# Transnormer attention and SoLU feed-forward on one core: chunk 5 on token rows, its scaling on GpSimd, and a new order of the pieces

## The chip, the cores and the metric

The kernel runs on one core of one Trainium2 chip. The metric is the device time of one execution in microseconds (us). Before the change it is 182.4 us, the median of three runs (181.66 to 182.57).

The core has five engines that run at once: TensorE (PE in the profile, with its weight loads shown apart as PEld), VectorE (DVE), ScalarE (ACT), GpSimd (POOL) and SyncE (SP), which here only issues transfers. Transfers run on 16 DMA engines; SP, ACT and POOL each have a queue for issuing them. The on-chip memory that all engines read is SBUF; matmuls write to PSUM, of which this kernel uses three slots of two banks (P0 to P2) and two slots of one bank (S0, S1).

## The reference

The inputs are q, k and v of shape (8, 8, 576, 64) (batch, head, position, head size). What is computed:

```
kv  = einsum('bhsd,bhse->bhde', k, v)            # one 64x64 matrix per head
o   = einsum('bhsd,bhde->bhse', q, kv)
x   = o / sqrt(mean(o*o over the 64) + 1e-6) * g_norm   # -> 4608 tokens x 512
h   = x @ w_in                                    # 512 -> 1024
u   = h * softmax(h)
y   = (u - mean(u)) / sqrt(var(u) + 1e-6) * g_ln
out = y @ w_out                                   # 1024 -> 512, float32
```

## The kernel before

The 4608 tokens are cut into nine chunks of 512. Chunks 0 to 7 are the first eight of the nine position groups of each batch; chunk 8 gathers the ninth group of all batches (`q_last`, filled by the copies `ql0` to `ql7`). Every chunk goes through the same stages, each a named piece:

- loads `k`, `v`, `q` (POOL queue, cast from float32 to bfloat16 under way; `k0a` and `v0a` come over SP and ACT and are cast by `cast0.0` and `cast0.1`). The number is the batch; `a` and `b` are the halves of batches 0 and 1;
- `kv` on PE makes the 64x64 matrices, `kc...` copies them to SBUF (`kvd`) in three parts: straight, and the two row halves swapped;
- q is turned, by PE (`qt`, copied out by `qc`) for chunks 0 to 4, by a DMA transpose on SP (`qx`) for chunks 5 to 8;
- `o` multiplies q with the matrices. For chunks 0 to 5 o comes out with features on partitions: `sq` squares it (ACT), `s` averages it over a head on PE, `ln` and `ex` give the reciprocal root (ACT), `x` scales (DVE). For chunks 6 to 8 (`ROWS_OF_X`) o comes out with tokens on partitions: `sq` (ACT), a row sum `vd` (DVE), two small ACT instructions `vl`, the spread of the scale factor `vg` (POOL, 128x1024), `x` (DVE, reads o from PSUM), and a DMA transpose `xt` on SP;
- `h` is the first big matmul; `e` the exponential (ACT), `u` the product (DVE). Chunks 0 to 2 keep features on partitions, with `r` (squares), `g` (sums) and the PE sums `z`. Chunks 3 to 8 have tokens on partitions: `e` and `u` give their sums along the way, `r` squares u for its sum (ACT or DVE), and `t` turns u by a DMA transpose on SP;
- `st` and `rs` make the last row factor, `a` is the second big matmul, `b` scales its result into a result buffer `ob` (ACT or DVE), `d` stores it.

All DMA transposes wait for `gate`, a one-element copy on POOL that needs the last load, `q7`.

The order is a table (`ORDER`) in which every piece stands once, with the buffer it takes after @ (M0 to M12 of 4.6 KB, L0 to L7 of 9.2 KB, `ob` of 2 KB a partition) and its engine after /. Each engine runs its own pieces in table order; waits between engines come from the data and the buffers. So a piece that is not ready holds up everything behind it on its engine or queue, and nothing else directly.

Lines in the profile: L314 `kv`, L359 `qt`, L370 `qx`, L407 `o` on features, L470 `o` on rows, L435 `s`, L495 `vg`, L504 `x` on rows, L483 `vd`, L512 `xt`, L572 and L581 `h`, L599 `e` on rows, L612 `u` on rows, L630 and L632 `r` on rows (ACT and DVE), L637 `t`, L767 and L774 `a`, L782 and L784 `b`, L173 and L175 copies by ACT and the others, L343 `gate`, L269 the loads, L714 to L720 the row statistics `st`.

Of the kernel before, what the change touches and what calls it, by code (L numbers as in the profile page):

```python
# [68 lines left out]
warm0@S0 k0a@L0,L1 v0a rsqrt q0a@M0 k0b ident qt0.0@S0 cast0.0/act cast0.1/dve kv0a@P0 kc0a.1/act v0b q0b wi0  # L69
kc0a.2/act gr warm1@S1 tg@S1 qc0.0/dve@M1 kc0a.0/act o0.0@P0 sq0.00@osq0 sq0.01@osq1 warm2@S0 kv0b@P1 kc0b.0/act  # L70
kc0b.1/dve s0.00@S0 ex0.00@rst0 kc0b.2/act qt0.1@P2 qc0.1/dve s0.01@S0 ex0.01@rst1 warm3@P1 o0.1@P2 sq0.10@osq1
sq0.11@osq0 warm4@S0 s0.10@S0 warm5@P1 gm@M2 x0.00@M1 ex0.10@rst0 s0.11@S1 x0.01 x0.10 ex0.11@rst1 x0.11 wi1
h0.0+@P0 wo0@L2 h0.1+ h0.2+@P1 h0.3+ h0.0 h0.1 h0.2 wo1@L3 table e0.0@M3 u0.0@L1 h0.4+@P2 k1a@L0 h0.5+ v1a h0.3 h0.4
# [784 lines left out]
```

## Time and profile before

The profiled execution took 181.77 us and spans 179.7 us from the first to the last instruction; 2.07 us lie around the span. The granted TensorE clock is 0.999.

| engine | busy us of 179.7 | instructions |
|---|---|---|
| PE | 164.9 | 1808 |
| PEld | 81.1 | 1831 |
| ACT | 128.1 | 239 |
| DVE | 127.1 | 222 |
| POOL | 71.9 | 83 |

The DMA engines moved 37.81 MB in 60424 packets. In the page's rows of 40 slices a digit is the busy share of a slice of 4.5 us in tenths. PE's matmuls overlap by some 160 ns each (379 ns from start to end, 216 ns from start to start), so that a group's time is not its count times its mean.

### The profile page before, as it was taken

The page shows a single profiled execution, that of the slowest core. Times are in us where ns is not written, and L with a number is a line of the kernel's source. Part 1 is how long each engine was busy: PE and PEld are TensorE (multiplying, and loading weights), DVE is VectorE, ACT ScalarE, POOL GpSimd, SP SyncE. Part 2 cuts the span into 40 slices and gives each one's busy share as a digit, 9 for nine tenths or more (in the row PEclk, how much of TensorE's full clock was granted, in tenths as well). Part 3 has the DMA queues.
Part 4 walks back from the last instruction along what each step waited for, and adds up shares of the span by engine and source line. Part 5 has one row for each costly group of instructions (what it writes and reads, how often), then busy time and mean ns, then how long its engine had stood idle before and what let it go on. Part 6 is the DMA issues. An engine that isn't in the chain of part 4 may idle for free.

```text
span 179.7 us, 4520 instructions
## 1 busy us (share of the span) xinstructions
PE 164.9 (92%) x1808; PEld 81.1 (45%) x1831; DVE 127.1 (71%) x222; ACT 128.1 (71%) x239; POOL 71.9 (40%) x83
## 2 busy tenths in 40 slices
PE   6899958699999999999998999899999999999990
...
ACT  2377794593899687979879898469979746986210
...
DMA  5999999999999999999799999999998689968994
GB/s 170 252 207 275 353 208 209 205 208 222 248 233 232 209 207 198 277 214 206 157 172 203 206 216 220 152 256 245 171 227 239 99 166 248 200 139 215 175 256 125
DMA packets 60424, 37.81 MB, mean 210 GB/s; under 512 B 42140, under 2 KB 55204, under 8 KB 60404
## 3 DMA queue, kind: packets, MB, share of 16 engines
...
## 4 chain that ended last, share of the span: by engine, by line
PE 63%; DMA 22%; DVE 6%; issue 3%; POOL 1%; SPq 1%; ACT 1%; POOLq 0%; DVEq 0%; ACTq 0%
PE ps_S L767 20%; PE ps_P L581 19%; DMA sb_M<-in_q_dram 9%; PE ps_P L572 8%; PE ps_P L767 5%; DMA out_dram<-sb_ob 4%; DMA sb_L<-in_v_dram 4%; DMA sb_M<-sb_M 3%; PE ps_S L359 2%; DVE sb_ob L784 2%; PE ps_P L314 2%; PE ps_P L407 2%; DMA sb_L<-sb_L 2%; PE ps_P L691 1%; PE ps_S L435 1%
## 5 line engine op out<-in xcount | busy, mean ns | idle before, releaser
L767 PE MATMUL ps_S<-w_out_sb,sb_L 128*128 128x512 bf16 x220 | 53.1, 379 | 2.9 <-issue 2.4
L581 PE MATMUL ps_P<-w_in_sb,sb_M 128*128 128x512 bf16 x188 | 42.7, 379 | 1.0 <-ACT kvd L173 0.8
L767 PEld LDWEIGHTS <-sb_L 128*128 128x128 bf16 x280 | 26.4, 98 | 33.4 <-issue 3.3
L612 DVE SCALAR_TENSOR_TENSOR sb_L<-ps_P,sb_M 128x1024 bf16<-128x1024 f32 x24 | 29.1, 1222 | 8.4 <-ACT sb_M L599 8.2
L599 ACT ACTIVATE sb_M<-ps_P 128x1024 f32<-128x1024 f32 x24 | 24.5, 1023 | 8.2 <-PE ps_P L581 7.1
L581 PEld LDWEIGHTS <-sb_M 128*128 128x128 bf16 x192 | 18.7, 98 | 23.3 <-issue 0.9
L495 POOL TENSOR_TENSOR sb_M<-rr,g_rep 128x1024 f32<-128x1024 f32 x6 | 12.3, 2061 | 30.4 <-ACT rr L491 23.7
L572 PE MATMUL ps_P<-sb_M,w_in_sb 128*128 128x512 bf16 x94 | 21.9, 379 | 0.1
L607 DVE TENSOR_TENSOR sb_L<-ps_P,sb_M 128x1024 bf16<-128x1024 f32 x12 | 14.6, 1222 | 8.2 <-ACT sb_M L592 8.2
L453 DVE SCALAR_TENSOR_TENSOR sb_M<-ps_P,g_cols,sb_rst 128x512 bf16<-128x512 f32 x24 | 18.0, 790 | 2.9 <-ACT sb_rst L443 2.6
L784 DVE TENSOR_SCALAR sb_ob<-ps_S,rstd 128x512 f32<-128x512 f32 (+1 forms) x19 | 13.8, 735 | 7.7 <-PE ps_S L767 2.2
L592 ACT ACTIVATE sb_M<-ps_P 128x1024 f32<-128x1024 f32 x12 | 12.2, 1024 | 6.9 <-PE ps_P L572 6.9
L643 POOL TENSOR_TENSOR sb_M<-sb_M 128x512 bf16<-128x512 f32 x12 | 15.1, 1278 | 4.9 <-ACT sb_M L592 4.8
L420 ACT ACTIVATE sb_osq<-ps_P 128x512 bf16<-128x512 f32 x24 | 13.4, 596 | 4.6 <-PE ps_P L407 4.6
L630 ACT ACTIVATE sb_M<-sb_L 128x1024 bf16<-128x1024 bf16 x14 | 14.6, 1047 | 0.0
L572 PEld LDWEIGHTS <-w_in_sb 128*128 128x128 bf16 x96 | 9.2, 98 | 10.5 <-issue 0.2
L801 POOL DMA_DIRECT2D out_dram<-sb_ob x10 | 6.3, 633 | 16.4 <-DVE sb_ob L784 8.8
L632 DVE SCALAR_TENSOR_TENSOR sb_M<-sb_L 128x1024 bf16<-128x1024 bf16 x10 | 12.8, 1276 | 0.1
L443 ACT ACTIVATE sb_rst<-sb_lss 128x512 f32<-128x512 f32 x20 | 12.0, 632 | 0.1
L767 PE MATMUL ps_P<-w_out_sb,sb_L 128*128 128x512 bf16 x47 | 11.4, 379 | 0.1
L206 PE MATMUL ps_S<-zeros 128*128 128x512 bf16 (+1 forms) x18 | 8.5, 591 | 1.8 <-DVE zeros L188 1.5
L624 POOL TENSOR_TENSOR sb_L<-sb_L 128x1024 bf16<-128x1024 bf16 x4 | 7.6, 1910 | 6.1 <-DVE sb_L L607 6.0
...
## 6 DMA issues: line engine op xcount, KB each, us to landing
out_dram<-sb_ob SPq DMA_DIRECT2D x14, 256.0 KB, 4.2
sb_L<-in_k_dram POOLq DMA_DIRECT2D x6, 576.0 KB, 12.2
sb_L<-in_v_dram POOLq DMA_DIRECT2D x6, 576.0 KB, 13.1
sb_M<-in_q_dram POOLq DMA_DIRECT2D x6, 576.0 KB, 12.3
out_dram<-sb_ob POOLq DMA_DIRECT2D x10, 256.0 KB, 4.8
...
```

What stands on the lines that cost most here:

```text
L420: nc.scalar.activation(out=t[:, :], in_=T["o", c, hf][:, z], func=AF.Square)
L453: nc.vector.scalar_tensor_tensor(out=T["x", c][:, pairs_of(c, hf), :, z], in0=T["o", c, hf][:, z].rearrange("p (n q) -> p n q", n=2), scal ...
L572: nc.tensor.matmul(t[:, f % 2], w_in_sb[:, dt, f * 128:(f + 1) * 128], T["x", c][:, dt].rearrange("p q z -> p (q z)"), start=(dt == 0), st ...
L581: nc.tensor.matmul(T["h", c, m][:, half], x_block(c, m, dt), w_in_sb[:, dt, half * 512:half * 512 + 512], start=(dt == 0), stop=(dt == NP ...
L599: nc.scalar.activation(out=t.rearrange("p a b -> p (a b)"), in_=T["h", c, m].rearrange("p a b -> p (a b)"), func=AF.Exp, accum_out=T["zsum ...
L607: nc.vector.tensor_tensor(out=flat(T["u", c][:, 2 * p:2 * p + 2, :]), in0=flat(T["h", c, p]), in1=flat(T["e", c, p]), op=MUL)
L612: nc.vector.scalar_tensor_tensor(out=T["un", c][:, m, :], in0=T["h", c, m].rearrange("p a b -> p (a b)"), scalar=1.0, in1=T["e", c, m].rea ...
L630: nc.scalar.activation(out=unused, in_=src, func=AF.Square, accum_out=by)
L632: nc.vector.scalar_tensor_tensor(out=unused, in0=src, scalar=1.0, in1=src, op0=MUL, op1=MUL, accum_out=by)
L643: nc.gpsimd.tensor_tensor(out=T["es", c][:, n, :], in0=e[:, 0, :], in1=e[:, 1, :], op=ADD)
L767: nc.tensor.matmul(T["acc", c, m][:, 0], T["u", c][:, f, m * 128:(m + 1) * 128], w_out_sb[:, f, :], start=(f == 0), stop=(f == NF - 1))
L784: nc.vector.tensor_scalar_mul(out=t[:, :], in0=src, scalar1=T["rstd", c][:, m:m + 1])
```

## The change

- `ROWS_OF_X` takes in chunk 5: its o, x and transpose take the token-row way.
- On token rows, x no longer reads PSUM. A new piece `oc` (ACT or DVE) copies o to an SBUF tile in float32, and `x` becomes a GpSimd multiplication of that tile with the spread factor.
- `kvd` becomes three tiles, one for each of the three copies.
- The row squares `r` of chunks 3 to 8 run on ACT only; the copies `ql` on POOL or ACT only; the row statistics `st` of chunks 3 to 8 become six small GpSimd multiplications and additions in place of four DVE instructions. The constants they need are two new small tiles.
- There are 9 instead of 8 L buffers and 11 instead of 7 result buffers.
- The order table is new throughout. By its engine marks, ten row squares leave DVE for ACT, two squares of chunks 0 to 2 leave ACT for POOL, `b` goes from 14 on ACT and 23 on DVE to 10 and 27, both first casts are on DVE, `ql` goes from 3 POOL, 3 DVE and 2 ACT to 5 POOL and 3 ACT, `oc` is 7 times on DVE and once on ACT. Loads 2 to 7 stand earlier, the first store (`d0.0`) stands behind the last load.

```diff
-SLOTS = {"P": 3, "S": 2, "L": 8, "M": 13, "osq": 4, "lss": 3, "rst": 4, "ob": 7}
+SLOTS = {"P": 3, "S": 2, "L": 9, "M": 13, "osq": 4, "lss": 3, "rst": 4, "ob": 11}
-ROWS_OF_X = (6, 7, 8)
+ROWS_OF_X = (5, 6, 7, 8)
 ORDER = """
...
-r0.1/act u0.2 u0.3 r0.2/act r0.3/act wm1 wc4 kv1a@P2 kc1a.1/act kc1a.0/act warm6@S0 qt1.0@S0 z0@P0 warm7@P1
-kc1a.2/act wc1 wc2 qc1.0/act@M1 o1.0@P2 warm8@S0 wc3 sq1.00@osq0 sq1.01@osq1 kv1b@P1 kc1b.1/act kc1b.2/act wc5 wc0
-wc7 y0 a0.00@S0 wc6 q1b k2@L5 v2 ql0/pool q2@M2 k3@L4 st0 rs0 qt1.1@S1 kc1b.0/dve s1.00@P0 s1.01@P1 ln1.00@lss0
...
-d0.0/pool q3@M1 s1.10@S0 ln1.10@lss1 x1.00@M7 x1.01 s1.11@P1 ln1.11@lss0 h1.0+@P2 h1.1+ ex1.10@rst0 x1.10
-ex1.11@rst1 x1.11 a0.20@S0 kv2@P1 kc2.1/dve kc2.2/dve a0.21 h1.0 h1.1 b0.1/act@ob1 d0.1/sp qt2.0@S1 kc2.0/dve
...
+ex0.10@rst2 x0.10 ex0.11@rst0 table x0.11 h0.0 h0.1 h0.2 h0.3 h0.4+@P1 h0.5+ h0.4 h0.5 wm0@S0 wm1 e0.0@M1 e0.1@M4
+u0.0@L1 k1a@L0 h0.6+@P0 v1a q1a@M5 k1b u0.1 e0.2@M6 h0.6 u0.2 h0.7+ h0.7 r0.0/act@L4 wc5 v1b q1b kv1a@P1 warm6@S1
+r0.1/act e0.3@M3 wc1 wc4 kc1a.0/act kc1a.2/act wc0 qt1.0@S1 warm7@P2 wc7 qc1.0/dve@M2 kc1a.1/act o1.0@P1 sq1.00@osq1
+sq1.01@osq0 u0.3 g0.0@M7 g0.1 warm8@S1 kv1b@P2 kc1b.1/act wc2 k2@L5 v2 q2@M4 k3@L6 wc6 s1.00@S1 s1.01@P0 wc3 g0.2
+kc1b.0/act ln1.00@lss0 ln1.01@lss1 ex1.00@rst0 ql0/act kc1b.2/dve r0.2/pool a0.00@S0 qt1.1@S1 g0.3 qc1.1/dve
+ex1.01@rst2 r0.3/pool z0@P0 x1.00@M0 y0 o1.1@P2 x1.01 a0.01 sq1.10@osq0 s1.10@S1 sq1.11@osq1 s1.11@P1 ln1.10@lss1
+ln1.11@lss0 st0 kv2@P0 kc2.0/dve a0.10@S1 a0.11 ex1.10@rst2 ex1.11@rst0 v3 q3@M3 k4@L2 v4 q4@M2 k5@L4 rs0 h1.0+@P1
...
+a1.00@S0 sq3.01@osq0 u2.3 rs1 a1.01 a1.10@S1 g2.2 g2.3 r2.2/pool r2.3/act s3.00@P2 ln3.00@lss0 ex3.00@rst2 q7@M8
...
+d0.1/pool d0.2/pool h3.21 e3.2@M10 kc7.0/dve kc7.1/dve kc7.2/dve a2.11 b2.1/dve@ob2 u3.2 s4.10@S1 gate@L0 t3.0 t3.1
+h3.30@P1 h3.31 sq4.11@osq1 ln4.10@lss0 ex4.10@rst1 x4.10 qx5@M11 a2.20@S1 s4.11@S0 a2.21 a2.30@P2 a2.31 e3.3@M6 u3.3
+ln4.11@lss0 ex4.11@rst1 x4.11 o5.0@P1 b2.2/dve@ob1 o5.1@P0 r3.2/act r3.3/act st3 sq5.0@rst1 a3.00@S0 a3.01
+sq5.1@rst2 b2.3/dve@ob0 a3.10@S1 oc5.0/dve@M11 oc5.1/act@M6 vd5.0 vd5.1 vl5.0 qx6@M12 o6.0@P1 oc6.0/dve@M10 o6.1@P2
+sq6.0@rst1 sq6.1@rst2 oc6.1/dve@M12 vd6.0 a3.11 h4.00@P0 h4.01 h4.10@P1 e4.0@M1 ql2/act u4.0@L6 h4.11 vd6.1 rs3
+b3.0/dve@ob9 b3.1/act@ob10 h4.20@P2 h4.21 vl5.1 e4.1@M4 d0.3/sp h4.30@P0 u4.1 d1.0/sp t3.2 a3.20@S1 h4.31 e4.2@M0
+u4.2 ql6/pool a3.21 vl6.0 b3.2/dve@ob4 vg5.0@M5 t3.3 a3.30@S0 a3.31 e4.3@M3 u4.3 d1.1/sp qx7@M9 o7.0@P2 o7.1@P1
+ql7/pool r4.0/act r4.1/act r4.2/act b3.3/dve@ob5 oc7.0/dve@M4 d1.2/pool d1.3/sp d2.0/pool d2.1/pool t4.0@L4 t4.1
+a4.00@S1 oc7.1/dve@M0 a4.01 r4.3/act ql4/pool ql5/pool a4.10@S0 a4.11 sq7.0@rst2 vg5.1@M2 x5.0@M7 x5.1 qx8@M8
+o8.0@P2 vg6.0@M9 x6.0@M3 xt5.0@M1 sq7.1@rst1 vd7.0 xt5.1 o8.1@P0 oc8.0/dve@M2 oc8.1/dve@M7 vd7.1 sq8.0@rst0
+sq8.1@rst2 st4 h5.00@P1 h5.01 e5.0@M9 u5.0@L0 h5.10@P2 vl6.1 vl7.0 xt6.0@M10 d2.2/sp d2.3/sp h5.11 h5.20@P0 h5.21
+h5.30@P1 e5.1@M8 e5.2@M6 u5.1 rs4 b4.0/dve@ob0 u5.2 vg6.1@M5 h5.31 vg7.0@M11 x6.1 r5.0/act vd8.0 h6.00@P2 h6.01 t4.2
+a4.20@S1 r5.1/act a4.21 e5.3@M9 vl7.1 t4.3 t5.0@L1 b4.1/dve@ob1 b4.2/dve@ob2 r5.2/act h6.10@P0 h6.11 t5.1 t5.2 u5.3
+e6.0@M5 u6.0@L6 vg7.1@M12 a4.30@S1 r5.3/act r6.0/act a4.31 x7.0@M6 a5.00@S0 xt6.1 x7.1 h6.20@P2 e6.1@M4 a5.01 vl8.0
+vd8.1 h6.21 vl8.1 e6.2@M5 b4.3/act@ob8 vg8.0@M11 u6.1 u6.2 h6.30@P1 h6.31 d3.0/sp xt7.0@M9 h7.00@P0 d3.1/sp h7.01
+h7.10@P2 d3.2/sp st5 e6.3@M10 t5.3 t6.0@L4 t6.1 u6.3 rs5 a5.10@S1 a5.11 x8.0@M0 e7.0@M12 xt7.1 xt8.0@M2 a5.20@P1
...
 """
-    kvd = big.tile([128, B, 2, 2, 2, D], BF16, name="kvd")
+    kvd = [big.tile([128, B, 2, 2, D], BF16, name=f"kvd{i}") for i in range(3)]
...
-        dst = kvd[:, b]
+        dst = kvd[part][:, b, ms].rearrange("p m x d -> p x m d")
...
+    def kv_of(b, n, swapped, half):
+        return kvd[1 + half if swapped ^ (n % 2) else 0][64 * half:64 * half + 64, b, n // 2, n % 2, :]
...
+    def o_out(c, hf, engine):
+        T["os", c, hf] = room(("os", c, hf), [128, 1024], FP32)
+        copy(engine, T["os", c, hf][:, :], T["o", c, hf].rearrange("p x i -> p (x i)"))
+
     def x_rows(c, hf):
...
-        nc.vector.tensor_tensor(
-            out=T["xr", c][:, hf], in0=T["o", c, hf].rearrange("p x i -> p (x i)"),
-            in1=T["rg", c, hf].rearrange("p i e -> p (i e)"), op=MUL,
+        nc.gpsimd.tensor_tensor(
+            out=T["xr", c][:, hf], in0=T["os", c, hf][:, :], in1=T["rg", c, hf].rearrange("p i e -> p (i e)"), op=MUL
         )
...
-                plan.add(f"r{c}.{m}", ("act", "dve"), lambda e, c=c, m=m: row_usq(c, m, e), [f"u{c}.{m}"],
+                plan.add(f"r{c}.{m}", ("act", "act"), lambda e, c=c, m=m: row_usq(c, m, e), [f"u{c}.{m}"],
...
+    def row_stats(c):
+
+        def product(name, in0, in1, op):
+            t = small.tile([128, 4], FP32, name=name)
+            nc.gpsimd.tensor_tensor(out=t[:, :], in0=in0[:, :], in1=in1[:, :], op=op)
+            return t
+
+        a = product("a", T["usum", c], T["usum", c], MUL)
+        a = product("a2", a, per_u, MUL)
+        d = product("d", T["zsum", c], T["zsum", c], MUL)
+        d = product("d2", d, per_z, MUL)
+        f = product("f", a, T["qsum", c], ADD)
+        T["vare", c] = product("vare", f, d, ADD)
```

111 lines of the change are left out of this document (41 added, 70 removed).

## The prediction

> **What bounds the kernel now.** I read the page first (busy shares, slices), then the waits of PE, then PE's timeline, then the DMA rows.
>
> ```profile
> PE 164.9 (92%) x1808; PEld 81.1 (45%) x1831; DVE 127.1 (71%) x222; ACT 128.1 (71%) x239; POOL 71.9 (40%) x83
> ...
> PE   6899958699999999999998999899999999999990
> ...
> ACT  2377794593899687979879898469979746986210
> ...
> DMA  5999999999999999999799999999998689968994
> ```
>
> PE is nearly always busy; DMA is full for the first half. VectorE, ScalarE and GpSimd have room on average. So a change gains only by less PE work, or by taking away waits of PE; whatever it moves off another engine is worth nothing by itself. The waits are few:
>
> ```profile
> PE ps_P L314 <- DMA sb_L<-in_v_dram: 1.6, 1, 1.6
> ...
> PE ps_P L581 <- ACT kvd L173: 0.8, 1, 0.8
> PE ps_P L407 <- DMA sb_M<-sb_M: 0.4, 1, 0.4
> ```
>
> PE's timeline places them, and gives the pace of its pieces:
>
> ```profile
> 26.26 0.48 PE L314 MATMUL ps_P<-sb_L 64*64 64x64 bf16 x36 [1.64 <-DMA sb_L<-in_v_dram]
> ...
> 27.57 0.62 PE L359 MATMUL ps_S<-ident,sb_M 128*128 128x128 bf16 x8 [0.30 <-DMA sb_M<-in_q_dram]
> ...
> 40.33 0.78 PE L314 MATMUL ps_P<-sb_L 64*64 64x64 bf16 x72
> ...
> 63.78 0.41 PE L407 MATMUL ps_P<-sb_M,kvd 64*64 64x256 bf16 x8
> 64.13 1.08 PE L691 MATMUL ps_P<-sb_L,stat_sel 128*32 128x128 bf16 x64
> ...
> 92.09 5.34 PE L581 MATMUL ps_P<-w_in_sb,sb_M 128*128 128x512 bf16 x24
> 97.81 0.41 PE L407 MATMUL ps_P<-sb_M,kvd 64*64 64x256 bf16 x8 [0.37 <-DMA sb_M<-sb_M]
> ...
> 104.25 0.95 PE L470 MATMUL ps_P<-kvd,sb_M 64*64 64x64 bf16 x64
> 105.14 0.39 PE L435 MATMUL ps_S<-sb_osq,head_mean 128*128 128x512 bf16 x1
> ...
> 115.72 8.79 PE L581 MATMUL ps_P<-w_in_sb,sb_M 128*128 128x512 bf16 x40 [0.75 <-ACT kvd L173]
> ```
>
> The 24 matmuls of 92.09 take (5.34 - 0.38)/23 = 0.216 us each, start to start; a half piece of `a` or `h` (four) is 0.86. From 115.72 on PE never waits by more than 0.2 us until its end.
>
> **PE's own work.** Chunk 5 loses its four `s` matmuls: 4 x 0.216 = 0.86. Its `o` goes from 2 x 0.35 (63.78 to 64.13) to 0.89 (104.25 to 105.14, two pieces): 0.19 more. Net -0.67, all on the path, as PE is the bound.
>
> **The two waits near 97.8 and 115.7: -1.12.** The second is `h5` behind a chain of copies into `kvd` that alternate between DVE and ACT; with a tile for each copy, and with `kv6` and `kv7` moved ahead of `o5`, nothing late writes there: -0.75. The first waits for `qx5`, which stands behind `gate`, which stands behind the last load:
>
> ```profile
> 36.00:40.00 4.00, 4.00 (x26) 1.82 (x26) 2.13 (x3) 3.63 (x9) 2.12 (x3) 1.00 1.22 209
> ...
> 70.94 0.75 POOL L269 DMA_DIRECT2D sb_M<-in_q_dram  x1 [0.47 <-PE ps_S L691]
> ...
> 88.83 0.18 POOL L343 COPY sb_L<-sb_M 1x1 bf16<-1x1 bf16 x1 [13.32 <-DMA sb_M<-in_q_dram]
> ...
> out_dram<-sb_ob SPq DMA_DIRECT2D x14, 256.0 KB, 4.2
> ...
> sb_L<-in_v_dram POOLq DMA_DIRECT2D x6, 576.0 KB, 13.1
> ```
>
> The last columns of the window row are DMA share (1.22) and GB/s (209): the loads run at the limit. A full load of 576 KB (0.59 MB) then takes 2.83 us, a half one 1.42. PE's `qt1.0` waited for `q1a` at 27.57. Behind it come k1b, v1b, q1b, then 18 full loads: 27.57 + 4.25 + 50.9 = 82.7. Before, `gate` opened at 88.83, as eight stores of 256 KB (`d0`, `d1`) lay in between: 6.1 us for eight, 0.8 each, which is what 256 KB take at a like rate. The new table puts all of them behind `q7`. Issuing the loads isn't what limits: the table has loads 2 to 5 behind one another, and the two buffers that come late (`k7` behind `a0`, `q7` behind `e2.3`) are asked for some 10 us ahead of their turn. `qx5` lets `o5.0` start 8.98 after `gate` (97.81 - 88.83), so at 91.7. When does PE get there? Ahead of `o5.0` the new order no longer has `h4` (8 x 0.86 = 6.9), but `kv6`, `kv7` (0.7 each by the row of 40.33) and half a piece of `a2` (0.86): 97.44 - 6.9 + 2.3 = 92.8, plus the 0.85 of the next part: 93.7. So the wait goes: -0.37. A gate 2 us later than 82.7 would bring it back; `a3`, which needs the first turned u, is behind it then.
>
> **The early order: +0.85.** `v1a` still sets `kv1a` at 26.26, since what stands ahead of it in the load queue is the same. But the new table has `kv2` earlier on PE: the old one has three more half pieces of `a0` and the first halves of `h1.0` and `h1.1` ahead of it, 4 x 0.86 = 3.5 us. By the rates above `v2` lands at 27.57 + 4.25 + 2 x 2.83 = 37.5; PE waits for it, and then has those 3.5 us still to do: 41.0, where the old order stands at `kv2` at 40.33. That is +0.65, whatever the pieces ahead of `kv2` do (`z0` now stands behind half an `a0` in place of warming matmuls, which saves waits that this one takes back). `qt3.0` is moved ahead likewise; `q3`, four loads behind `v2`, lands at 48.8, about when PE asks: I take +0.2, between 0 and 0.65. The start:
>
> ```profile
> 5.96 1.15 ACT L173 CAST sb_L<-sb_L 128x1152 bf16<-128x1152 f32 x1 [3.40 <-DMA sb_L<-in_k_dram]
> 6.31 0.97 DVE L175 CAST sb_L<-sb_L 128x1152 bf16<-128x1152 f32 x1 [4.16 <-DMA sb_L<-in_v_dram]
> ```
>
> With both casts on DVE the second ends at 5.96 + 2 x 0.97 = 7.9 in place of 7.3: 0.6 later. I cost it at nothing, because the 1.64 wait ahead of `kv1a` covers it; with that cover gone it costs 0.6.
>
> **What moves between the other engines.**
>
> ```profile
> L630 ACT ACTIVATE sb_M<-sb_L 128x1024 bf16<-128x1024 bf16 x14 | 14.6, 1047 | 0.0
> ...
> L632 DVE SCALAR_TENSOR_TENSOR sb_M<-sb_L 128x1024 bf16<-128x1024 bf16 x10 | 12.8, 1276 | 0.1
> ...
> L443 ACT ACTIVATE sb_rst<-sb_lss 128x512 f32<-128x512 f32 x20 | 12.0, 632 | 0.1
> L439 ACT ACTIVATE sb_lss<-ps_S 128x512 f32<-128x512 f32 x13 | 7.7, 598 | 0.8 <-PE ps_S L435 0.7
> ...
> L504 DVE TENSOR_TENSOR sb_M<-ps_P,sb_M 128x1024 bf16<-128x1024 f32 x6 | 7.2, 1215 | 0.0
> L483 DVE TENSOR_REDUCE ms<-sb_rst 128x16 f32<-128x1024 bf16 x6 | 7.2, 1212 | 1.2 <-ACT sb_rst L479 1.2
> ...
> L801 POOL DMA_DIRECT2D out_dram<-sb_ob x10 | 6.3, 633 | 16.4 <-DVE sb_ob L784 8.8 <-ACT sb_ob L782 7.6
> L479 ACT ACTIVATE sb_rst<-ps_P 128x1024 bf16<-128x1024 f32 x6 | 6.0, 1016 | 1.1 <-PE ps_P L470 1.1
> ...
> L630 ACT ACTIVATION_READ_ACCUMULATOR sb_M<-sb_L 128x1 f32 x14 | 2.7, 192 | 0.0
> ...
> L175 POOL COPY q_last<-sb_M 128x256 bf16<-128x256 bf16 x3 | 2.3, 760 | 0.0
> ```
>
> ACT: ten squares come (10 x 1.24 = 12.4), four `ln` and four `ex` of chunk 5 go (4 x 1.23 = 4.9); with four `b`, two early squares and a cast gone as well, less than the +7.5 of these two terms is left. DVE loses ten squares (12.8) and six `x` (7.3) and pays seven `oc` at about an L504 each (8.5): some -11. Both are off PE's path as long as no single piece comes late. POOL's rows:
>
> ```profile
> 107.92 1.90 POOL L495 TENSOR_TENSOR sb_M<-rr,g_rep 128x1024 f32<-128x1024 f32 x1 [15.98 <-ACT rr L491]
> ...
> 138.08 6.65 POOL L495 TENSOR_TENSOR sb_M<-rr,g_rep 128x1024 f32<-128x1024 f32 x3 [6.11 <-ACT rr L491]
> ...
> 139.28 1.78 DVE L632 SCALAR_TENSOR_TENSOR sb_M<-sb_L 128x1024 bf16<-128x1024 bf16 x1
> ...
> L495 POOL TENSOR_TENSOR sb_M<-rr,g_rep x6: 1892/1901/2878, 107.9 to 142.8; 128x1024 f32<-128x1024 f32 x6
> ...
> DMA to landing us min/median/max: 4.2/4.7/5.2
> ```
>
> GpSimd has no row for `x`. Its nearest is L495 (two operands, 1024 columns): 1.90 alone, 2.88 at worst beside a DVE square (1.78 in place of 1.28). I take 1.90, as the squares leave DVE, and keep 2.88 as the upper end. A small statistics step lies near the one-element copy of `gate` (0.18), at most at half a `ql` (0.38): six in a row make 1.1 to 2.3 us. They stand ahead of the chunk's `rs` and `b`, not of its `a`. Queued behind them on POOL are `vg6.1` (`st4`), `x8.0` (`st5`) and `vg8.1` with `x8.1` (`st6`, which itself waits for the last square of chunk 6 on ACT); by the table the first of these waits for its `vl` anyway, and `h8` asks for the others some 10 us of PE work later: nothing, and the 2.3 us each where that cover is gone.
>
> The path to look at is `o5` to `h5`. After `o5.0` starts (93.7) the new order has four chunks of `o` (4 x 0.89), `a3` (6.9), half of `a4` (3.5) and `h4` (6.9) on PE before `h5.00`: 20.9 us, so it is asked for at 114.6. The chain: `o5.0` done 94.1; `sq` 1.3 later, as two squares of chunk 3 stand ahead on ACT: 95.4; `sq5.1` and `oc5.1` (1.0 each) while `vd` runs: 97.4; `vl`, two instructions near the 0.19 of an accumulator read: 97.8. Then on POOL, in order, two `vg` and `x5.0` (3 x 1.90), three `ql` (2.3), three stores (1.9): 107.7. `xt5.0` behind `qx8` on SP, about 1, and 4.7 to landing (the last quoted row is that of the six `xt`): 113.4. That leaves 1.2 us. The same count for `h7.00`, whose `x7.0` is queued on POOL behind `vg7.1`, which waits for a `vl` that stands behind four row pieces on ACT, leaves nothing. I take +0.3 for such handovers together: at least 0; at most 3.8, with POOL's pieces at 2.88 (1.8 at `h5`, 2 x 0.98 at `h7`).
>
> Two more transposes and the eight deferred stores come to the DMA's second half, whose slices show 6 to 9 where the first half has only 9: hidden; a turn that lands late costs some 0.5 (5.2 against 4.7 in the landing row).
>
> [...]
>
> **Sum.** 181.77 (this execution; 0.6 below the median of 182.4) - 0.67 - 1.12 + 0.85 + 0.3 = 181.1. The tail after PE's last matmul (`b`, two stores) is unchanged.
>
> **Rivals.** (1) Slower: GpSimd sets the pace of the late chunks. For: it now does four 128x1024 pieces a chunk besides statistics and stores; against: 40% busy before. At 2.88 a piece the handovers cost 3.8 in place of 0.3: 184.6. From 2.4 us a piece (5 x 0.5 - 1.2 = 1.3) the gain is gone. [...] (2) Slower: ACT, with all row squares, becomes the order that PE waits for. For: it holds `e`, `sq`, `vl`, `rs` and `r` in one line, and a `vl` or `rs` that waits for another engine holds up the next `e`; against: 71%. Its 12.4 us of squares fall into some 65 us in which the trace has it 8 tenths busy: where PE waits for half a square (0.6) once in each of the last three chunks, 181.1 + 1.8 = 182.9. (3) The gate gains nothing: stores or a late `q7` hold `qx5`, and the new wait at `kv2` eats the rest: 181.77 - 0.67 + 0.85 + 0.3 = 182.2. (4) More gain: no wait at `kv2` (loads faster than I count) and no handover waits: 181.1 - 0.85 - 0.3 = 180.0 or less.
>
> **Chances.** Forecast 0.44, (4) 0.10, (3) 0.13, (1) 0.20, (2) 0.13. The range from 179.4 to 184.8 takes in (4) with 0.6 for the start, and (1). The forecast's own range is 180.4 to 182.0. A difference of 0.5% (0.9 us) is about what a measurement can tell here; by it the forecast is faster for 0.36 of its 0.44, (4) wholly, (3) same: faster 0.46, same 0.21, slower 0.33.
>
> **What the profile would show.** `gate` at 82 to 84, no wait before `o5.0` or `h5`; a PE wait for a load at `kv2` near 36; L495 and the new `x` near 1.9 to 2.1; POOL above 55%; PE gaps before `h5.00` and `h7.00` under 0.5. It is wrong if the gate opens after 85, if POOL's pieces exceed 2.3, or if PE waits repeatedly on ACT after 95.

## The result, and the profile after

The changed kernel took 190.16 us (median of 4, 189.06 to 191.0) against 182.49 for the kernel before on the same chip: 1.042 times as long, 95% interval 1.036 to 1.049. I had forecast 181.1 and a range up to 184.8. It is slower, by more than any of my rivals gave. The profiled execution spans 188.1 us (179.7 before): 8.4 to explain. Executions more than 1.5% over the fastest of the same kernel (one each of e4, e5, e7 and e14, two of e15, three of e9) are left out of the medians and ratios below.

The page of the changed kernel first: busy time by engine, then slices.

```profile
PE 169.3 (90%) x1875; PEld 82.0 (44%) x1875; DVE 114.3 (61%) x181; ACT 130.3 (69%) x248; POOL 105.9 (56%) x138
...
PE   6879997699999999899998898979999999499990
...
PEclk9999999999999999999999999999999999889998
```

VectorE lost 12.8 us of work, GpSimd gained 34, and none of that shows in the time. New are a slice of PE at 4 tenths, the 35th, from 160 us on, and a granted clock of 8 tenths in that slice and the next. The waits of PE that were not there before:

```profile
PE ps_P L590 <- DMA sb_M<-sb_M: 2.5, 1, 2.5
...
PE ps_P L590 <- DVE sb_L L621: 1.8, 2, 1.4
...
PE ps_P L475 <- DMA sb_M<-q_last: 0.7, 1, 0.7
```

The timeline of PE in the changed kernel places them. L590 is `h` of token rows, L475 `o` of token rows, L776 `a`.

```profile
102.35 1.89 PE L590 MATMUL ps_P<-w_in_sb,sb_M 128*128 128x512 bf16 x8 [0.69 <-ACT sb_rst L484]
104.58 1.89 PE L590 MATMUL ps_P<-w_in_sb,sb_M 128*128 128x512 bf16 x8 [0.34 <-DVE sb_M L175]
106.84 1.02 PE L590 MATMUL ps_P<-w_in_sb,sb_M 128*128 128x512 bf16 x4 [0.38 <-DVE sb_L L621]
...
117.07 1.20 PE L475 MATMUL ps_P<-kvd,sb_M 64*64 64x64 bf16 x64 [0.69 <-DMA sb_M<-q_last]
...
125.19 3.61 PE L590 MATMUL ps_P<-w_in_sb,sb_M 128*128 128x512 bf16 x16 [1.39 <-DVE sb_L L621]
...
162.41 1.57 PE L590 MATMUL ps_P<-w_in_sb,sb_M 128*128 128x512 bf16 x4 [2.52 <-DMA sb_M<-sb_M]
163.77 1.91 PE L776 MATMUL ps_S<-w_out_sb,sb_L 128*128 128x512 bf16 x4
```

The last line is the slow clock, granted at 0.50 from 163.70 to 165.50: four matmuls in 1.70 us (163.77 to 165.47), where four take 0.86.

The two orders differ, so times of the same name can't be subtracted. What can be is the lag: when PE starts a piece, less the work that its table has put ahead of that piece (pieces counted, at the durations of the prediction's rows, the same for both).

| PE at | work ahead, before / after | start, before / after | lag, before / after | the changed kernel behind by |
|---|---|---|---|---|
| `kv2` | 32.2 / 28.8 | 40.3 / 38.5 | 8.1 / 9.8 | 1.6 |
| `o5.0` | 87.2 / 82.6 | 97.8 / 94.8 | 10.6 / 12.2 | 1.6 |
| `a4.20` | 112.7 / 112.1 | 124.4 / 128.6 | 11.7 / 16.6 | 4.9 |
| `h8.20` | 146.4 / 143.2 | 158.3 / 162.4 | 11.9 / 19.2 | 7.4 |
| PE's end | 162.9 / 162.2 | 174.9 / 183.3 | 12.0 / 21.0 | 9.1 |

So 1.6 us are lost in the start, 3.3 between 95 and 129 (the lag grows by 4.4 there, and by 1.1 in the kernel before), 2.5 at one wait before `h8.20`, 1.7 to the slow clock behind it, and 0.65 are won by less work: 8.4.

### The profile page after: what moved, and what is told of

Its sections match the earlier page's. It is cut to its first block, busy times and chain, and to the rows that moved or that the text cites. A ratio compares the mean times of both kernels' runs of the same rounds, so it can differ in the third digit from the quotient of the medians.

```text
span 188.1 us, 4634 instructions
## 1 busy us (share of the span) xinstructions
PE 169.3 (90%) x1875; PEld 82.0 (44%) x1875; DVE 114.3 (61%) x181; ACT 130.3 (69%) x248; POOL 105.9 (56%) x138
## 4 chain that ended last, share of the span: by engine, by line
PE 56%; DMA 19%; DVE 7%; ACT 6%; issue 5%; POOL 3%; SPq 1%; DVEq 0%; ACTq 0%; POOLq 0%
PE ps_S L776 20%; PE ps_P L590 15%; DMA sb_M<-in_q_dram 8%; PE ps_P L581 7%; DMA sb_M<-sb_M 7%; PE ps_P L776 6%; DMA sb_L<-in_v_dram 4%; POOL sb_M L500 2%; PE ps_S L364 2%; DVE sb_M L175 2%; PE ps_S L700 1%; ACT sb_M L608 1%; DVE kvd L175 1%; PE ps_P L319 1%; ACT sb_M L639 1%
## 5 line engine op out<-in xcount | busy, mean ns | idle before, releaser
L776 PE MATMUL ps_S<-w_out_sb,sb_L 128*128 128x512 bf16 x232 | 56.4, 384 | 0.5 <-DVE w_out_sb L760 0.5
L590 PE MATMUL ps_P<-w_in_sb,sb_M 128*128 128x512 bf16 x192 | 45.8, 384 | 5.8 <-DMA sb_M<-sb_M 2.5
L776 PEld LDWEIGHTS <-sb_L 128*128 128x128 bf16 x280 | 26.8, 99 | 33.5 <-issue 3.2
L590 PEld LDWEIGHTS <-sb_M 128*128 128x128 bf16 x192 | 18.7, 99 | 30.3 <-issue 6.7
L639 ACT ACTIVATE sb_M<-sb_L 128x1024 bf16<-128x1024 bf16 x24 | 25.0, 1045 | 2.3 <-DVE sb_L L621 2.3
L793 DVE TENSOR_SCALAR sb_ob<-ps_S,rstd 128x512 f32<-128x512 f32 (+1 forms) x23 | 16.6, 724 | 10.7 <-PE ps_S L776 5.4
L581 PE MATMUL ps_P<-sb_M,w_in_sb 128*128 128x512 bf16 x96 | 22.0, 379 | 0.0
L500 POOL TENSOR_TENSOR sb_M<-rr,g_rep 128x1024 f32<-128x1024 f32 x8 | 15.2, 1900 | 10.1 <-ACT rr L496 9.5
L513 POOL TENSOR_TENSOR sb_M<-sb_M,sb_M 128x1024 bf16<-128x1024 f32 x8 | 18.8, 2359 | 0.2
L601 ACT ACTIVATE sb_M<-ps_P 128x1024 f32<-128x1024 f32 x12 | 12.2, 1023 | 6.4 <-PE ps_P L581 6.4
L458 DVE SCALAR_TENSOR_TENSOR sb_M<-ps_P,g_cols,sb_rst 128x512 bf16<-128x512 f32 x20 | 15.0, 786 | 1.2 <-ACT sb_rst L448 0.6
L581 PEld LDWEIGHTS <-w_in_sb 128*128 128x128 bf16 x96 | 9.0, 98 | 11.2 <-issue 1.5
L808 POOL DMA_DIRECT2D out_dram<-sb_ob x12 | 6.4, 538 | 12.4 <-ACT sb_ob L791 11.4
L274 POOL DMA_DIRECT2D sb_M<-in_q_dram x10 | 7.5, 752 | 7.8 <-DMA sb_L<-in_k_dram 2.5
L633 POOL TENSOR_TENSOR sb_L<-sb_L 128x1024 bf16<-128x1024 bf16 x6 | 11.3, 1888 | 0.0
L488 DVE TENSOR_REDUCE ms<-sb_rst 128x16 f32<-128x1024 bf16 x8 | 9.6, 1213 | 2.5 <-ACT lv L494 2.3
L484 ACT ACTIVATE sb_rst<-ps_P 128x1024 bf16<-128x1024 f32 x8 | 7.8, 1013 | 4.7 <-DVE sb_M L175 4.7
```

Of the source, the lines that this page charges most:

```text
L458: nc.vector.scalar_tensor_tensor(out=T["x", c][:, pairs_of(c, hf), :, z], in0=T["o", c, hf][:, z].rearrange("p (n q) -> p n q", n=2), scal ...
L500: nc.gpsimd.tensor_tensor(out=t[:, :, :], in0=T["rr", c, hf][:, :, None].to_broadcast([128, 16, D]), in1=g_rep[:, None, :].to_broadcast([1 ...
L513: nc.gpsimd.tensor_tensor(out=T["xr", c][:, hf], in0=T["os", c, hf][:, :], in1=T["rg", c, hf].rearrange("p i e -> p (i e)"), op=MUL)
L581: nc.tensor.matmul(t[:, f % 2], w_in_sb[:, dt, f * 128:(f + 1) * 128], T["x", c][:, dt].rearrange("p q z -> p (q z)"), start=(dt == 0), st ...
L590: nc.tensor.matmul(T["h", c, m][:, half], x_block(c, m, dt), w_in_sb[:, dt, half * 512:half * 512 + 512], start=(dt == 0), stop=(dt == NP ...
L639: nc.scalar.activation(out=unused, in_=src, func=AF.Square, accum_out=by)
```

## The experiments

All ratios are to the kernel before, measured beside the run. "Changed" and the numbers of e1 to e5 and e8 go with the changed kernel's 190.16.

| run | median us | ratio, 95% interval |
|---|---|---|
| e1 changed, x on VectorE | 189.15 | 1.037 (1.034 to 1.041) |
| e2 changed, x8.1 ahead of chunk 6's statistics | 185.54 | 1.017 (1.013 to 1.021) |
| e3 changed, two stores behind x8.1's transpose | 188.19 | 1.033 (1.029 to 1.037) |
| e4 changed, four buffers for the small tiles | 188.58 | 1.032 (1.024 to 1.040) |
| e5 changed, square and copy by bank | 190.58 | 1.041 (1.031 to 1.051) |
| e6 before, turned k^T v in three tiles | 182.01 | 0.999 (0.996 to 1.002) |
| e7 before, x on GpSimd from copies | 190.79 | 1.045 (1.038 to 1.052) |
| e8 changed, seven squares on VectorE | 191.77 | 1.053 (1.045 to 1.061) |
| e9 before, stores deferred | 184.32 | 1.009 (1.006 to 1.013) |
| e10 = e2 + e4 | 184.53 | 1.011 (1.007 to 1.014) |
| e11 before, chunk 5 on token rows | 185.07 | 1.016 (1.010 to 1.022) |
| e12 = e10 + chunk 6's squares first | 184.76 | 1.015 (1.009 to 1.022) |
| e13 = e12 + last queries' transpose sooner | 189.74 | 1.040 (1.032 to 1.047) |
| e14 before, copies only, x on VectorE | 189.06 | 1.038 (1.030 to 1.046) |
| e15 = e7 + squares and statistics off VectorE | 194.97 | 1.070 (1.057 to 1.083) |
| e16 = e10 + x on VectorE | 186.83 | 1.026 (1.018 to 1.034) |

### Is it GpSimd's pace? (e1)

My first rival. In the changed kernel, the two GpSimd groups of a row chunk (L500 is the scale, L513 the new x):

```profile
L500 POOL TENSOR_TENSOR sb_M<-rr,g_rep 128x1024 f32<-128x1024 f32 x8 | 15.2, 1900 | 10.1 <-ACT rr L496 9.5
L513 POOL TENSOR_TENSOR sb_M<-sb_M,sb_M 128x1024 bf16<-128x1024 f32 x8 | 18.8, 2359 | 0.2
```

x takes 2.36 us, not the 1.90 that I took. Edit:

```diff
-        nc.gpsimd.tensor_tensor(
+        nc.vector.tensor_tensor(
             out=T["xr", c][:, hf], in0=T["os", c, hf][:, :], ...
```

> The changed kernel, with x of the token-row chunks back on VectorE, still from the SBUF copy of o. Theory Q (queues: the late pieces stand behind others that wait, on ACT, DVE and SP): the waits of PE ahead of h4 stay, and the last transpose of x stays behind a store on SP that waits for b6.0, so 188.5 to 190.5 us against 190.2. Theory G (GpSimd's pace: x took 2.36 us there, not 1.90): eight x of 2.36 leave GpSimd for eight of 1.2 on VectorE, the PE waits of 1.4 near 125 and 2.5 near 162 go, and with them the slower clock: 186 us or less.

189.15, theory Q's case: 1.0 us less, with intervals that overlap. The wait at 162 went down to 0.68, but a new one of 1.84, for x5's transpose, came up before `h5.00`, and the matmuls behind it were slow (24 took 6.69 us, where 24 take 5.34 in the kernel before), so part of the gain was lost again. Moving x off GpSimd is worth about 1 us of 7.7.

### The wait before `h8.20` (e2, e3)

The chain of work that ended last in the changed kernel, at that place:

```profile
152.40 0.59 ACT sb_ob L791
153.01 0.47 SPq L808
153.54 0.58 SPq L808
154.23 8.13 DMA sb_M<-sb_M
162.41 1.57 PE ps_P L590 x4
```

The transpose of x8.1 is issued at 154.23, behind the store `d6.0`, which waits for `b6.0` on ScalarE; and it takes 8.13 us to land. GpSimd's timeline says what went on meanwhile (L723 statistics, L808 and L810 stores):

```profile
147.05 0.20 POOL L723 TENSOR_TENSOR f<-a,qsum 128x4 f32<-128x4 f32 x1 [4.40 <-ACT sb_M L639]
...
149.45 2.35 POOL L513 TENSOR_TENSOR sb_M<-sb_M,sb_M 128x1024 bf16<-128x1024 f32 x1
151.75 1.90 POOL L810 DMA_DIRECT2D out_dram<-sb_ob  x3
153.64 3.17 POOL L808 DMA_DIRECT2D out_dram<-sb_ob  x6
```

Chunk 6's statistics stand ahead of chunk 8's x and wait 4.40 us for a square on ScalarE; behind x8.1, nine stores that have piled up (of chunks 4 and 5, not the eight that the new order puts off) go out at once, just as the transpose does. e2 moves the statistics, e3 the two stores on SyncE:

```diff
# e2, in the table
- st6 rs6 vg8.1@M10 x8.1
+ vg8.1@M8 x8.1 st6 rs6
# e3, in the table
- d5.3/sp d6.0/sp ... xt8.1
+ xt8.1 d5.3/sp d6.0/sp
```

> The changed kernel, with the statistics of chunk 6 behind the last spread and the last x on GpSimd's queue (and the last spread in buffer M8, which is free, so that it doesn't wait for a square either). x8.1 then ends near 146 in place of 151.8. Theory G or one of GpSimd's order: xt8.1 lands before h8.20 asks, the wait of 2.5 us goes: 187 us. Theory Q: xt8.1 still stands on SP behind the store d6.0, which waits for b6.0 until 153: no gain, 189.5 to 190.7 us.

> The changed kernel, with the stores d5.3 and d6.0 behind the transpose xt8.1 on SP; nothing else. Theory Q: xt8.1 is issued when x8.1 ends (151.8) in place of 154.2; the wait of PE near 162 shrinks from 2.5 to 0.5 or less and the granted clock stays near 1.00: 186.5 to 188.3 us. Theory G, or a theory that the deferred stores slow the transpose on the DMA engines whatever its place: the transpose lands as late as before, 189.5 us or more.

e2: 185.54, 4.6 us less and below both ranges; by theory Q I had expected nothing, since the issue on SyncE should have stayed late. It did stay late. SyncE and GpSimd in e2, with PE's `h8.20` (L589 there):

```profile
155.09 1.39 SPq L519 DMA_TRANSPOSE sb_M<-sb_M  x1
```

```profile
147.88 1.90 POOL L809 DMA_DIRECT2D out_dram<-sb_ob  x3
149.77 3.17 POOL L807 DMA_DIRECT2D out_dram<-sb_ob  x6
```

```profile
160.14 1.03 PE L589 MATMUL ps_P<-w_in_sb,sb_M 128*128 128x512 bf16 x4
161.01 1.03 PE L775 MATMUL ps_S<-w_out_sb,sb_L 128*128 128x512 bf16 x4
```

How long the eight transposes of x (L520; L519 in e2) took to land, in the changed kernel and then in e2:

```profile
DMA to landing us min/median/max: 3.1/3.1/8.1
```

```profile
DMA to landing us min/median/max: 3.1/3.1/3.8
```

The issue is 0.9 later than before (155.09), but the nine stores went out 3.9 us sooner (147.88), and the slowest transpose landed in 3.8 us instead of 8.1. The four stores that stand ahead of this transpose on SyncE are the same in both. PE doesn't wait, and its matmuls keep their pace: the four after it take 0.86. So the statistics cost by holding nine stores back into the transpose's time.

e3: 188.19. SyncE's transpose, then GpSimd's first stores, in e3:

```profile
151.92 1.23 SPq L520 DMA_TRANSPOSE sb_M<-sb_M  x1
```

```profile
151.84 1.90 POOL L810 DMA_DIRECT2D out_dram<-sb_ob  x3
```

The transpose goes out at 151.92, along with the first of the same stores, and still lands in at most 3.3 us. So stores beside it aren't enough; the one that took 8.13 us was issued some 2.5 us into the burst, behind stores that had already gone out. The wait and the slow matmuls are gone too (four in 0.86 again), but only 2.0 us are saved: the stores on SyncE now hold up the turns of u7 and u8, and the last piece waits.

```profile
179.20 1.92 PE L783 MATMUL ps_S<-w_out_sb,sb_L 128*128 128x256 bf16 x16 [1.74 <-DMA sb_L<-sb_L]
```

### The wait at 125 (e4), and both repairs (e10)

`h5.30` waits for u5.0, which stands on VectorE behind a head sum (L488) that needs one of the two buffers of the small tiles `ms`; the earlier of them is read by a ScalarE piece that is queued behind a square, which waits for a copy:

```profile
122.78 1.22 DVE L488 TENSOR_REDUCE ms<-sb_rst 128x16 f32<-128x1024 bf16 x1 [2.26 <-ACT lv L494]
```

```diff
-        T["ms", c, hf] = small.tile([128, 16], FP32, name="ms")
+        T["ms", c, hf] = small.tile([128, 16], FP32, name="ms", bufs=4)
# and the same for rr
```

> The changed kernel, with four small buffers in place of two for the row sums and for the scale factors. The DVE reduction vd7.1 then no longer waits (2.3 us) until the ACT instructions vl6.1 have read an old sum. Theory Q: u5.0 comes 1.2 us earlier, the wait of PE near 125 shrinks from 1.4 to about 0.2, and the time falls by 0.5 to 1.4 us, to 188.8 to 189.7. Theory G: nothing, 190.2.

> The changed kernel with the last scale and x of chunk 8 ahead of chunk 6's statistics on GpSimd and with four buffers for the small tiles. If the two repairs are for two separate stalls they add: 185.5 less 1.3, 184.2 (183.7 to 184.9). If the wait at 125 is only passed on to the next: 185.2 to 185.8.

e4: 188.58, and the wait of 1.39 is gone. The time alone doesn't show a gain, as e4's interval overlaps the changed kernel's; the trace does, and so does e10 on top of e2. e10: 184.53, inside the bounds for "they add" (183.7 to 184.9): 5.6 us less than the changed kernel. In e10, PE's `a4.20` starts at 127.43 (lag 15.4) and PE ends at 177.96 (lag 15.7): behind `a4.20` nothing is lost any more. What stays is the start and the part from 95 to 118.

### Square and copy of one PSUM tile (e5, e6, e12)

Every row chunk's `o` is now read twice from PSUM, by ScalarE's square (L484) and VectorE's copy (L175). The changed kernel's ScalarE and VectorE near chunk 6:

```profile
101.27 1.94 ACT L484 ACTIVATE sb_rst<-ps_P 128x1024 bf16<-128x1024 f32 x2 [1.79 <-DVE sb_M L175]
```

```profile
100.02 1.22 DVE L175 COPY sb_M<-ps_P 128x1024 f32<-128x1024 f32 x1
103.30 1.22 DVE L175 COPY sb_M<-ps_P 128x1024 f32<-128x1024 f32 x1 [2.06 <-issue]
```

The square starts 0.03 us after the copy of the same tile ends (101.24), the next copy 0.09 after the next square (103.21): one after the other, though both only read. My chain didn't have the copy on VectorE between them at all. The added copy lengthens the handovers: 4.7 us of ScalarE's waits, in three, are for L175, though not all of it is this order (one of the copies had itself waited 0.81 for PE).

```profile
ACT sb_rst L484 <- DVE sb_M L175: 4.7, 3, 2.4
```

e5 splits square and copy by bank:

```diff
-        nc.scalar.activation(out=t[:, :], in_=T["o", c, hf].rearrange("p x i -> p (x i)"), func=AF.Square)
+        for z in range(2):
+            nc.scalar.activation(out=t[:, 512 * z:512 * z + 512], in_=T["o", c, hf][:, z], func=AF.Square)
# and the same for o_out's copy
```

> The changed kernel with each square of token rows (ScalarE) and each copy of o (VectorE) as two instructions, one to a PSUM bank. Theory R (two engines that read one PSUM tile are put one after the other, so the added copy makes square and copy a chain): if the order goes by bank, a copy starts when its own bank has been squared, a pair of them ends about 0.8 us sooner, the waits between L484 and L175 shrink, and the time is 0.5 to 1.5 us under 190.2: 188.7 to 189.7. If the order goes by the whole tile, only the fixed cost of ten more instructions on each engine shows and the time is 190 to 191. Rival (the chain of square and copy is covered anyway): 190.2 within 0.3, with shorter waits and no earlier h5.00.

190.58, the case of "by the whole tile". ScalarE and VectorE in e5 at the same place:

```profile
101.78 2.06 ACT L485 ACTIVATE sb_rst<-ps_P 128x512 bf16<-128x512 f32 x4 [1.92 <-PE ps_P L592]
```

```profile
103.93 1.29 DVE L175 COPY sb_M<-ps_P 128x512 f32<-128x512 f32 x2 [2.25 <-issue]
```

The two halves of a copy still wait until all four half squares are done (103.84). Whether two banks read at the same time would pay was not shown, because in e5 too the readers took turns by tile.

e6 takes the same question to the part of the change that has a tile for each copy of the turned k^T v:

```diff
-    kvd = big.tile([128, B, 2, 2, 2, D], BF16, name="kvd")
+    kvd = [big.tile([128, B, 2, 2, D], BF16, name=f"kvd{i}") for i in range(3)]
# kv_copy and kv_of as in the change
```

> The kernel before with one part of the change alone: the turned k^T v in three tiles, one for each copy. My prediction's step: the 0.75 us wait ahead of h5 goes, about 181.7. Theory R: the copies by VectorE and ScalarE still read one PSUM tile and still go one after the other, so nothing moves: 182.4 within 0.3.

182.01, the same within 0.3%, and the wait that I had said would go is still there (L581 is `h`):

```profile
PE ps_P L581 <- ACT kvd L173: 0.7, 1, 0.7
```

So it isn't the one SBUF tile that makes the copies alternate. That they read one PSUM tile is what is left, and is not shown by itself.

e12, on top of e10, puts chunk 6's squares ahead of its copies and chunk 5's head sums behind both:

```diff
- vd5.0 vd5.1 vl5.0 qx6@M12 o6.0@P1 oc6.0/dve@M10 o6.1@P2 sq6.0@rst1 sq6.1@rst2 oc6.1/dve@M12 vd6.0
+ qx6@M12 o6.0@P1 sq6.0@rst0 oc6.0/dve@M10 o6.1@P2 sq6.1@rst3 oc6.1/dve@M12 vd5.0 vd5.1 vl5.0 vd6.0
```

> The kernel of e10_after_e2_e4 with chunk 6's squares ahead of its copies, in two other buffers, and chunk 5's head sums behind them on VectorE. Theory R (the order of square and copy of one PSUM tile holds the banks of o6, for which h4.1 and h4.2 wait): the waits of 0.83 and 0.34 go, 183.4 to 184.1 against 184.5. Rival (the waits are covered by the one for the last queries' transpose at 117.4): that wait grows from 1.0 to about 2 and the time stays 184.5 within 0.4.

184.76, no gain: the rival's time, but not by its mechanism, as the wait ahead of `o8` fell to 0.39. The waits of 0.83 and 0.34 went, and one of 1.69 for u4.0 came in their place, as the head sums now stand ahead of it on VectorE. Two things were changed at once here, so this doesn't part the order of square and copy from the work that the copies give VectorE; it shows that this order only moves the wait. An order without that cost wasn't found.

### The queue of transposes (e13)

The transpose of the last queries goes out behind two turns of u4, though SyncE stands idle for 3.5 us ahead of these.

```diff
- ... t4.0@L4 t4.1 ... ql4/pool ql5/pool ... qx8@M8
+ ... ql4/pool ql5/pool ... qx8@M8 t4.0@L4 t4.1
```

> On top of e12: the copies of the last queries sooner on GpSimd and their transpose on SyncE ahead of the two of chunk 4's u, in 3.5 us in which that queue waits for VectorE. The wait of 1.0 (or, by e12's rival, 2) ahead of o8 goes: 182.6 to 183.6. If x5's transposes are then the next to be late (chunk 5's handover), h5.00 waits for one by as much and the time is e12's.

189.74, 5 us worse than e12; neither case had that. PE in e13 (L774 is `a4.0`):

```profile
117.13 6.51 PE L774 MATMUL ps_S<-w_out_sb,sb_L 128*128 128x512 bf16 x16 [4.19 <-DMA sb_L<-sb_L]
```

SyncE in e13, the last queries' transpose (L373) ahead of the turns of u4 (L644):

```profile
107.10 3.55 SPq L373 DMA_TRANSPOSE sb_M<-q_last  x1
110.83 5.19 SPq L644 DMA_TRANSPOSE sb_L<-sb_L  x2
```

The transpose keeps the queue for 3.55 us, so that the turns of u4 begin at 110.83. PE waited 4.19, and the 16 matmuls after it took 6.51 instead of 3.63. The wait ahead of `o8` did go.

### One part alone in the kernel before (e7, e14, e15, e9, e11)

e7 takes x of chunks 6 to 8 to GpSimd from copies made by VectorE, e14 makes the copies but leaves x on VectorE, e15 adds to e7 the change's last edit (squares on ScalarE, statistics on GpSimd):

```diff
# e7
-        nc.vector.tensor_tensor(out=T["xr", c][:, hf], in0=T["o", c, hf]..., in1=T["rg", c, hf]..., op=MUL)
+        nc.gpsimd.tensor_tensor(out=T["xr", c][:, hf], in0=T["os", c, hf][:, :], in1=T["rg", c, hf]..., op=MUL)
- sq6.0@rst0
+ sq6.0@rst0 oc6.0/dve@M13          (and so behind each of the six squares)
# e14: e7 with nc.vector.tensor_tensor
# e15: e7 with r3.* to r8.* on act, row_stats as in the change
```

> The kernel before, in its own table, with x of chunks 6 to 8 on GpSimd from copies made by VectorE (three more medium buffers); nothing else. Theory Q (the loss is made by the new order of the queues and the stores, not by GpSimd's x): GpSimd is at 2.36 us a piece in six pieces, with the prologue of the three chunks 10 us ahead of their matmuls in the old table; 182.4 to 183.5. Theory G (x on GpSimd is late by its nature): 184.5 or more, with waits of TensorE for the transposes of x7 and x8.

> The kernel before with the six copies of o added on VectorE and x made on VectorE from the copies: no work moved to GpSimd. VectorE has 7.2 us more. If the copies are what costs in e7 (their place on VectorE, and in series with the squares): 187 to 191, near e7's 190.8. If GpSimd's pace is (2.36 for 1.2 a piece, and what it holds up): 183 to 185.5.

> e7 with the squares of chunks 3 to 8 on ScalarE and the statistics on GpSimd, so that VectorE has no late work on SBUF alone but the head sums. In e7 VectorE's square took 2.76 us and a 128x4 product 1.82 us beside a running GpSimd instruction (1.28 and 0.16 in the kernel before). If that is what costs: 185 to 188. If ScalarE, which takes on 10 us, or the chain of square and copy is: 189.5 to 192.

e7 takes 190.79, 8.7 us over the kernel before beside it (182.12). That is theory G's time, but not its waits: PE waits 2.77 us for a `b`, 1.74 for a copy of the turned k^T v and 1.60 for a u, and not for x7 or x8. e14 takes 189.06, 7.2 over (181.89), so such a loss comes without any x on GpSimd. It is not a share of e7's loss, since in e14 VectorE makes the copies and x, where in e7 a copy stands in for x (and two x from copies on VectorE took 4.05 us in e14, where the next took 1.22). VectorE in e14 (L788 is `b`, L483 the head sum):

```profile
137.46 2.34 DVE L175 COPY sb_M<-ps_P 128x1024 f32<-128x1024 f32 x2
139.72 2.33 DVE L483 TENSOR_REDUCE ms<-sb_rst 128x16 f32<-128x1024 bf16 x2
142.37 1.23 DVE L175 COPY sb_M<-ps_P 128x1024 f32<-128x1024 f32 x1 [0.32 <-ACT sb_rst L479]
143.51 0.74 DVE L788 TENSOR_SCALAR sb_ob<-ps_S,rstd 128x512 f32<-128x512 f32 x1
```

```profile
144.30 3.61 PE L771 MATMUL ps_S<-w_out_sb,sb_L 128*128 128x512 bf16 x16 [2.88 <-DVE sb_ob L788]
```

Three copies and two head sums stand ahead of the scaling that frees PE's output bank, and the last copy waits for the square behind it in ScalarE's queue. PE waits 2.88 us. I take it for the same kind of loss as in the changed kernel at another place, where the new table spreads the copies but pays for them between 95 and 129; that is argued, not shown. What the copies cost there alone could not be tried, since without them the tiles of `o` stay occupied until x, and this order has given them to `h4` by then.

e15 takes 194.97, worse than e7 by 4.2 (on another chip) and outside both ranges, in part by the mechanism of e2: on GpSimd the statistics wait 5.33 us for a square on ScalarE, the stores queued behind them go out at 169.58, VectorE's `b` waits for one of the seven output buffers until 173.69, and PE then waits 2.00 for that `b`. A wait of 3.16 us at 146.49, like the 2.77 of e7, is not of that kind. VectorE's waits in e15:

```profile
DVE sb_ob L792 <- DMA out_dram<-sb_ob: 10.1, 2, 6.8
```

And GpSimd's:

```profile
168.80 0.20 POOL L722 TENSOR_TENSOR f<-a,qsum 128x4 f32<-128x4 f32 x1 [5.33 <-ACT sb_M L638]
...
169.58 2.15 POOL L807 DMA_DIRECT2D out_dram<-sb_ob  x4 [0.30 <-issue]
```

So the change's eleven buffers may be part of what lets it put statistics there. Still, the hold-up that the last edit avoids is there; VectorE in e7, beside GpSimd's x and scale (144.69 to 149.89 and 152.27 to 154.17), where the square had taken 1.28 and a 128x4 product 0.16 in the kernel before:

```profile
145.37 2.76 DVE L636 SCALAR_TENSOR_TENSOR sb_M<-sb_L 128x1024 bf16<-128x1024 bf16 x1
...
152.37 1.82 DVE L724 SCALAR_TENSOR_TENSOR vare<-f,d 128x4 f32<-128x4 f32 x1
```

e9 defers the stores of chunks 0 and 1 behind the gate, with eleven buffers; e11 has chunk 5 on token rows with x by VectorE from PSUM:

```diff
# e9
- "ob": 7          + "ob": 11
- d0.* d1.* ahead of the gate
+ gate@L3 t3.0 t3.1 qx5@M10 d0.0/pool d0.1/sp d0.2/sp d0.3/sp ... t3.3 d1.0/sp d1.1/sp d1.2/sp d1.3/pool
# e11
- ROWS_OF_X = (6, 7, 8)
+ ROWS_OF_X = (5, 6, 7, 8)
- o5.0@P1 sq5.00@osq0 sq5.01@osq1 ... x5.10 x5.11
+ o5.0@P1 sq5.0@rst0 vd5.0 ... vl5.0 vg5.0 ... x5.0 xt5.0 vl5.1 vg5.1 ... x5.1 xt5.1
```

> The kernel before with eleven output buffers and the stores of chunks 0 and 1 put behind the gate, one part of the change alone. If the stores hold up the loads, the gate opens 1 to 5 us before 88.83 and the wait of 0.37 ahead of o5.0 goes: 181.7 to 182.3. Theory B (the deferred stores come back as a burst on the DMA engines, beside the transposes): the gate opens earlier but transposes of chunk 3 or x land later, and the time is 182.4 to 184.

> The kernel before with chunk 5 on token rows and nothing else: x by VectorE from PSUM, three more medium buffers, its own table. TensorE has 0.67 us less to do; the banks of o5 are held longer and two more transposes go out near 105. If chunk 5 is harmless: 181.5 to 182.6. If the held banks or the transposes stop TensorE: 183 to 185, with a wait of h4 or kv6 for a PSUM tile.

e9: 184.32, 2.0 slower than the kernel before and just over theory B's range. Its gate, and PE's wait for the turned u of chunk 4:

```profile
87.40 0.18 POOL L343 COPY sb_L<-sb_M 1x1 bf16<-1x1 bf16 x1 [15.63 <-DMA sb_M<-in_q_dram]
```

```profile
111.88 1.90 PE L767 MATMUL ps_S<-w_out_sb,sb_L 128*128 128x512 bf16 x8 [1.96 <-DMA sb_L<-sb_L]
```

The gate opens 1.4 us sooner than at 88.83, not 6, and what was put off comes back beside the transposes. e11: 185.07, 2.7 slower than 182.33: PE waits 1.27 ahead of one piece of `o` for a u on VectorE, and 1.32 ahead of another for x5, which holds its PSUM tile. It was not harmless, as I had half expected; by my own sum it should have gained 0.67.

### The last edit, and x once more (e8, e16)

```diff
# e8, changed kernel; r4.3 r5.0 r5.1 r6.1 r7.2 r8.2 r8.3
-  r6.1/act
+  r6.1/dve
# e16: e10 with nc.vector.tensor_tensor for x
```

> The changed kernel with seven late squares back on VectorE (r4.3, r5.0, r5.1, r6.1, r7.2, r8.2, r8.3), as many as before. ScalarE has then about 8 us less after 108, VectorE about 9 us more. Theory A (ScalarE's order after 108 is what makes u, st6 and x8.1 late): 188 to 189.5, with st6's wait for ScalarE shorter by over 1 us. Theory Q (the order on GpSimd and the stores' burst make it): 189.8 to 191, because r6.3 stays on ScalarE and VectorE's copies of o come later.

> The kernel of e10_after_e2_e4 with x back on VectorE from the copies (e1's edit on top). If GpSimd's pace still costs its 1 us: 183.2 to 184.0. If the two repairs took that 1 us with them, or VectorE's 9.6 us of x now come ahead of u: 184.3 to 186.

e8: 191.77, 1.6 more than the changed kernel, with intervals that overlap a little, and above both ranges. The wait of `st6` did shrink, from 4.40 to 2.62 us, and the time rose all the same: the late squares are better on ScalarE here. A square beside x took 2.23 us, the next 1.21.

e16: 186.83, 2.3 more than e10, above its higher range. With the two stalls repaired, x is better on GpSimd than on VectorE; that the 1 us of e1 was part of these stalls is argued.

## Why the prediction was wrong

- **PE's own work, -0.67:** stands; the tables' work differs by 0.65.
- **The two waits near 97.8 and 115.7, -1.12:** both waits are gone. But the gate opened at 84.74 and not at 82.7, and it was no load that it waited for:

```profile
84.74 0.18 POOL L348 COPY sb_L<-sb_M 1x1 bf16<-1x1 bf16 x1 [11.41 <-PE ps_P L319]
```

  It writes into the buffer that `kv6` has to leave. The reason "with a tile for each copy" was wrong (e6). That `kv6` and `kv7` come earlier is what is left to have taken the wait away; it was not run alone.
- **The early order, +0.85:** 1.6. In the changed kernel's trace PE does not wait for v2. It stands 1.79 us inside the sums `z0`, for something that the profile doesn't name, and then starts `kv2` at 38.50 without a wait:

```profile
36.27 0.40 PE L700 MATMUL ps_P<-sb_M,stat_sel 128*32 128x128 bf16 x14 [1.79 <-issue]
```

  In e1 and e5, which lack that gap, PE waits 1.30 and 1.56 us for v2, to 38.36 and 38.71. So v2 came 0.9 to 1.2 us later than the 37.5 that I counted, and either cause alone holds `kv2` to about 38.5. The cause of the gap stays open; the kernel before has one of 1.73 too, in `a0.00` at 33.73.
- **What moves between the other engines (x at 1.90):** 2.36, within the bounds that I kept. It was the wrong thing to look at: about 1 us by e1, less than nothing by e16.
- **The handovers, +0.3 (0 to 3.8):** this is the step that failed. I followed one chain, `o5` to `h5`, left `oc5.0` on VectorE out of it, and priced only GpSimd's pieces for the rest. `h5.00` itself did not wait. What waited were pieces of `h4` and `h5` that no chain of mine held: 0.69 for a square of o6's tile, 0.34 for a copy, 0.38 and 1.39 for a u behind head sums on VectorE; `o8` waited 0.69 for its transpose. That is 3.5 of the 4.4 us by which the lag grows from 95 to 129; with the two old waits gone, 1.1, the net is 3.3. With four small buffers in place of the two, which I hadn't looked at, `a4.20` starts 1.2 sooner (e10). That the copies, and the squares that wait for them, are the cause of the rest is argued from the queues; no run takes the copies out of this order.
- **The statistics on POOL, "nothing, and the 2.3 us each where that cover is gone":** the second failure. I saw that `st6` waits for the last square of chunk 6 and that x8.1 stands behind it, but priced the six small instructions and not the wait (4.40), nor the nine stores that are queued behind x8.1. e2 and e3 show that this is what made the transpose late.
- **The DMA's second half, "a turn that lands late costs some 0.5":** one turn took 8.13 us, against 5.2 as the worst of before. With the slow clock behind it this and the last point are 4.2 us, and e2, which mends them together, is worth 4.6.
- **The rivals:** (1) named GpSimd for its pace; it was its order. (2) had PE wait for ScalarE three times by 0.6; the wait for a square is one of 0.69, and the square that `st6` waits for is on ScalarE too. (3) and (4) don't fit: the gate opened early, both old waits went, and the time rose. None had stores and transposes meeting, or two readers of one tile.

In sum: I had -0.6, and 8.4 came. Of the 9 between them, 0.8 is in the start (1.6 against 0.85), 4.1 in the handovers (4.4 against 0.3) and 4.2 in the statistics and the late transpose (against nothing).

What stays open: 2.2 us of e10, from the start and from 95 to 118. e12 and e13 moved that loss without removing it. No version tried beats the kernel before; e6 equals it.
